# Attention outputs stored with channels as rows: transposes moved from TensorE to VectorE in a parallel attention and MLP block

## The chip, the cores and the metric

The kernel runs on one core of one Trainium2 chip. The metric is device time in microseconds (us), the median of several executions. Trace rows name the engines PE (TensorE, matmuls), PEld (its weight loads), DVE (VectorE), ACT (ScalarE), POOL (GpSimd) and SP (SyncE, which here only issues DMAs). A "q" behind an engine means its instruction queue: SPq rows are DMA issues.

## The reference

The input x is 2048 tokens of 576 channels in float32. It is layer-normed once, and two branches are added to it: a sliding, dilated attention (32 heads of 18 channels; each token sees 8 keys at distances 0, 2, ..., 14) with an output projection, and a dense layer with Mish between 576 and 4608 channels.

```python
xn = layernorm(x)
q, k, v = split_heads(xn @ wqkv)                  # 32 heads of 18
logits = einsum("bhsd,bhswd->bhsw", q, kg) * 18 ** -0.5   # kg: keys at pos - 2*w, w < 8
o = einsum("bhsw,bhswd->bhsd", softmax(logits), vg)
attn = o.reshape(1, 2048, 576) @ wo
h = xn @ w1 + b1
mlp = (h * tanh(softplus(h))) @ w2
out = x + attn + mlp
```

## The kernel before

Tokens are handled in two halves `hf` of 1024 (`SH`). Token `p * 8 + j` of a half lies on partition p (128) in row group j (`TJ` = 8). Every float32 matrix product is made from a high part in fp32r and a low part (the remainder), three products for one; most of the large products also go by a seven-product scheme over 2x2 blocks, which is why the code forms sums and differences of operands (S1 to S4, T1 to T4).

The order of the work is written out by hand. `add` appends items to `plan`, each a stretch of TensorE work (a QKV item, a part of the first dense product, a pair of the second, a part of the output projection); `before` hangs other work in front of an item (loads, casts, steps of attention). At the end every engine's instructions are chained in that order, so each engine and SP's one DMA queue run strictly in program order: an instruction that waits holds all behind it on its queue.

Attention is a generator (`attention`, line 511) advanced at chosen items. It handles the 16 head-pair units of a half two at a time, eight pairs in each half, 16 in all. For each pair POOL multiplies queries and keys, VectorE reduces them to logits, softmax follows, POOL multiplies by the values (`pv`), and VectorE reduces these into `og`, a tile of 128 partitions by 8 row groups by 72 channels (line 582). After the last of the four reductions of a pair, SP stores `og` in the DRAM buffer `o_d` (line 584), with tokens as rows: 1024 pieces of 72 floats. The first half's pairs end between 142 and 636 us, the second half's between 706 and 1058.

The output projection runs last: eight blocks p of 256 tokens (row groups j and j + 1 of a half; blocks 0 to 3 are the first half). `o_load` (line 880) brings row group j as a tile `o` of 128 tokens by 576 channels, with the last 64 channels doubled behind, in two DMAs. `o_split` (line 888) turns it and prepares the operands for TensorE in steps: step 0 takes row group j + 1 into `t1`, step 1 takes row group j into `t0` and the last channels of both into `tr_`, each by TensorE transposes of 128x128 into PSUM; ScalarE casts the high parts (A, B, S), VectorE and POOL form the sums and the low parts. The steps of block p + 1 are placed inside the three parts of block p (`wo_part`, line 1042); block 0's stand ahead, among the last items of the dense layer. Each part multiplies into one of three PSUM banks h1, h3, h2 and VectorE adds the result to the output tile (`acc`, line 1064); h1 is multiplied into again after it has been read, so a product there waits for the addition before it. SP loads block p + 2's tiles while block p runs, and sends the finished rows out. `A` and `B` of successive blocks share a ring of three buffers ("wb").

Of the kernel before, what the change touches and what calls it, by code (L numbers as in the profile page):

```python
# [8 lines left out]
F32 = mybir.dt.float32  # L9
# [30 lines left out]
def block_kernel(ctx: ExitStack, tc: tile.TileContext, x, wq, wo, w1, b1, w2, mask, out):  # L40
# [470 lines left out]
    def attention(hf):  # L511
# [9 lines left out]
        for pair in range(NQ * UQ // PU):  # L521
            n = f"{hf}_{pair}"
            vs, nxt = [], []
            L = sb.tile([P, PU, TJ, W, 2], F32, tag="L", bufs=2, name=f"L_{n}")
            hj = TJ // 2
            for k, (kt, q) in enumerate(kqs):
                for c in range(2):
                    flush()
                    pr = sb.tile([P, hj, W, CU], F32, tag="pr", bufs=2, name=f"pr_{n}_{k}_{c}")
                    j0 = c * hj  # L530
                    hh = hj // 2
                    on = hf and pair == 0
                    if on:
                        nc.vector.tensor_tensor(
                            out=pr, in0=q[:, j0:j0 + hj, None, :].to_broadcast([P, hj, W, CU]),
                            in1=win(kt, 0, CU, j0, hj), op=ALU.mult)
                    for x in () if on else range(0, hj, hh):
                        nc.gpsimd.tensor_tensor(  # L538
                            out=pr[:, x:x + hh], in0=q[:, j0 + x:j0 + x + hh, None, :].to_broadcast([P, hh, W, CU]),
                            in1=win(kt, 0, CU, j0 + x, hh), op=ALU.mult)  # L540

                    def red(pr=pr, k=k, j0=j0, L=L):
                        nc.vector.tensor_reduce(  # L543
                            L[:, k, j0:j0 + hj].rearrange("p j w h -> p (j w h)"),
                            pr.rearrange("p j w (h d) -> p (j w h) d", h=2), axis=AX, op=ALU.add)
                    behind[0] = red
                    if k == 0:
                        vs.append(load_kv(hf, pair * PU + c, 1))
                    yield
            flush()  # L550
            if hf == 0:
                lm = L[0:2].rearrange("p k j w h -> p k (j w h)")
                nc.vector.tensor_add(lm, lm, mk[:, None, :].to_broadcast([2, PU, TJ * W * 2]))
            m = sb.tile([P, PU * TJ, 2], F32, tag="m", bufs=2, name=f"m_{n}")
            Lf = L.rearrange("p k j w h -> p (k j) w h")
            Lt = Lf.rearrange("p j w h -> p j h w")
            nc.vector.tensor_reduce(m, Lt, axis=AX, op=ALU.max)
            mb = m[:, :, None, :].to_broadcast([P, PU * TJ, W, 2])
            nc.vector.tensor_sub(Lf, Lf, mb)
            Ls = L.rearrange("p k j w h -> p (k j w h)")  # L560
            if (hf, pair) == (0, 4):
                soon.append(lambda: nc.scalar.preload_act_table_set("natural_log_exp_and_others"))
            soon.append(lambda Ls=Ls: nc.scalar.activation(Ls, Ls, AF.Exp, scale=SCALE))
            if (hf, pair) == (0, 4):
                soon.append(root1)
            yield
            nc.vector.tensor_reduce(m, Lt, axis=AX, op=ALU.add)
            nc.vector.reciprocal(m, m)
            nc.vector.tensor_mul(Lf, Lf, mb)  # L569
            og = sb.tile([P, TJ, PU * CU], F32, tag="og", bufs=1, name=f"og_{n}")  # L570
            for k, vt in enumerate(vs):
                for h in range(2):
                    flush()
                    pr = sb.tile([P, TJ, DH, W], F32, tag="pr", bufs=2, name=f"pv_{n}_{k}_{h}")
                    for x in range(0, TJ, hj):
                        nc.gpsimd.tensor_tensor(  # L576
                            out=pr[:, x:x + hj].rearrange("p j d w -> p j w d"),
                            in0=L[:, k, x:x + hj, :, h:h + 1].to_broadcast([P, hj, W, DH]),
                            in1=win(vt, h * DH, DH, x, hj), op=ALU.mult)

                    def red(pr=pr, og=og, c0=k * CU + h * DH, last=(k, h) == (PU - 1, 1), pair=pair):
                        nc.vector.tensor_reduce(og[:, :, c0:c0 + DH], pr, axis=AX, op=ALU.add)  # L582
                        if last:
                            nc.sync.dma_start(
                                o_d[hf][:, pair * PU * CU:(pair + 1) * PU * CU]
                                .rearrange("(p j) c -> p j c", j=TJ), og)
                    behind[0] = red
                    if (hf, pair, k, h) == (0, *(4, 0, 1)):
                        newton1()
                    if k == 0 and (pair + 1) * PU + h < NQ * UQ:  # L590
                        nxt.append(load_kq(hf, (pair + 1) * PU + h))
                    yield
            kqs = nxt
        flush()
        yield

    ASTEPS = NQ * UQ // PU * 9

# [281 lines left out]
    def o_load(hf, j):  # L880
        if j >= TJ or (hf, j) in os_:
            return
        o = os_[hf, j] = sb.tile([P, 5 * P], F32, tag="xn", bufs=XNB, name=f"o_{hf}_{j}")
        ov = o_d[hf].rearrange("(p j) d -> p j d", j=TJ)[:, j, :]
        nc.sync.dma_start(o[:, 0:D], ov)
        nc.sync.dma_start(o[:, D:D + 64], ov[:, KT * P:D])

    def o_split(p, step, early=False):
        hf, j = divmod(2 * p, TJ)
# [12 lines left out]
        H = 2 * P  # L902
        if step == 0:
            src = os_[hf, j + 1]
            for k in range(KT):
                nc.tensor.transpose(t1[:, k * P:(k + 1) * P], src[:, k * P:(k + 1) * P], ident)
            a21 = od["a21"] = sb.tile([P, H], F32, tag="mn", bufs=5, name=f"a21_{p}")
            nc.scalar.copy(a21, t1[:, 0:H])
            s1 = od["s1"] = sb.tile([P, 2, H], F32, tag="mn", bufs=5, name=f"s14_{p}")
            nc.vector.tensor_tensor(out=s1[:, 0], in0=t1[:, H:2 * H], in1=a21, op=ALU.add)  # L910
            a22 = t1[:, H:2 * H].rearrange("p (k t) -> p k t", k=2)
            nc.scalar.copy(B[:, 0], a22)
            nc.vector.tensor_sub(B[:, 1], a22, B[:, 0].bitcast(F32))
            return
        a1, s1 = od["a21"], od["s1"]
# [2 lines left out]
        rr = tr_[:, 0:H].rearrange("p (k t) -> p k t", k=2)  # L918
        if step == 1:
            src = os_[hf, j]  # L920
            for k in range(KT):
                nc.tensor.transpose(t0[:, k * P:(k + 1) * P], src[:, k * P:(k + 1) * P], ident)
            for k in range(2):
                nc.tensor.transpose(tr_[:, k * P:(k + 1) * P], os_[hf, j + k][:, KT * P:], ident)
            s2 = od["s2"] = sb.tile([P, 2, H], F32, tag="mn", bufs=5, name=f"s23_{p}")
            nc.vector.tensor_tensor(out=s2[:, 0], in0=s1[:, 0], in1=t0[:, 0:H], op=ALU.subtract)
            nc.vector.tensor_tensor(out=s2[:, 1], in0=t0[:, 0:H], in1=a1, op=ALU.subtract)
# [199 lines left out]

    kv_d = [dram.tile([2 * UQ, HALO + S, CU], F32, name=f"kv_d{g}") for g in range(NQ)]
    q_d = [dram.tile([UQ, S, CU], F32, name=f"q_d{g}") for g in range(NQ)]
    o_d = [dram.tile([SH, D], F32, name=f"o_d{h}") for h in range(NH)]  # L1130
    y_d = dram.tile([SH, D], F32, name="y_d")

    def rest_loads():
# [455 lines left out]
```

## Time and profile before

| | |
|---|---|
| time, three runs | 1119.57 us median (1119.29 to 1120.29) |
| profiled execution | span 1118.2 us from the first to the last instruction, 18402 instructions; the profile has no other time of it |
| SP's stores of `og` | 16, 0.51 to 0.76 us each to issue |
| SP's loads of `o` | 32 (two for each of 16 tiles), 0.32 to 0.78 us each to issue |
| TensorE transposes of `o` | 80, in lines 906, 922 and 924 |
| DMA | 271.08 MB, 147487 packets, of which 30114 under 512 B |

In a profile's group rows ("line engine op out<-in ... xcount | busy, mean ns | idle before"), the middle is the total busy time in us and the mean of one in ns; the end is the time for which the engine stood idle just before these instructions and what ended most of it. Waiting lists read "who line <- what it waited for: us in total, times, longest". The chain in order of time and the timeline start each row with the start in us and the length in us; equal neighbours are merged, with their count behind an x. A row by source has min/median/max in ns.

### The profile page before, as it was taken

To read this page: it belongs to the slowest core of one execution; us is meant where nothing else is said; L and a number is where in the kernel's file an instruction comes from. 1 tells how busy PE (TensorE), PEld (TensorE's weight loads), DVE (VectorE), ACT (ScalarE), POOL (GpSimd) and SP (SyncE) were. 2 spreads that over 40 slices of the span, in tenths; PEclk is the share of its full clock that TensorE was granted. 3 is DMA by queue.
4 is the path that set the end of the run, shared out by engine and by line. 5 is a ranking of instruction groups with operands and counts; after the bars stand their busy time and mean duration, and the time that the engine had idled before them with its cause. 6 is when DMAs were issued, how large, how long until landed. Compare 5 with 4: busy or idle time off the path is not lost.

```text
span 1118.2 us, 18402 instructions
## 1 busy us (share of the span) xinstructions
PE 1109.2 (99%) x6630; PEld 1023.9 (92%) x6630; DVE 835.2 (75%) x1355; ACT 491.7 (44%) x892; POOL 777.4 (70%) x631
## 2 busy tenths in 40 slices
PE   8999999999999999999999999999999999999998
PEld 8999899999999999999999888989999999999998
DVE  6369788888888888887656566687866677776876
ACT  5544645544554545555233354343433343443332
POOL 2479777767689687685787346666789878668632
PEclk9999999999999999999999999999999999999999
DMA  6899695868767849666696797665655477576463
GB/s 200 284 311 313 227 357 205 294 227 282 260 241 265 273 169 342 226 240 215 208 332 234 240 378 254 225 200 188 220 192 190 173 266 270 207 258 243 160 217 108
DMA packets 147487, 271.08 MB, mean 242 GB/s; under 512 B 30114, under 2 KB 86724, under 8 KB 147396
## 3 DMA queue, kind: packets, MB, share of 16 engines
q1 hardware_dynamic: 147396, 269.91, 69.8%
q8 instruction: 52, 0.85, 0.3%
q14 instruction: 39, 0.32, 0.1%
HBM read 160.39 MB, written 109.48 MB: 241 GB/s over the span
## 4 chain that ended last, share of the span: by engine, by line
PE 94%; DVE 3%; POOL 1%; ACT 1%; issue 1%; DMA 0%; SPq 0%; DVEq 0%; POOLq 0%; ACTq 0%
PE h L661 30%; PE po L759 20%; PE pq L348 11%; PE po L872 10%; PE po L851 7%; PE h L667 6%; PE o L1060 4%; PE z L446 4%; POOL accP L860 1%; DVE accP L875 0%; POOL act L713 0%; DMA acc<-in_x 0%; PE ta L75 0%; DVE og L582 0%; POOL act L814 0%
## 5 line engine op out<-in xcount | busy, mean ns | idle before, releaser
L759 PEld LDWEIGHTS po<-w,act 128*128 128x128 f32 x1728 | 236.4, 188 | 6.0 <-POOL act L713 0.4
L759 PE MATMUL po<-w,act 128*128 128x288 f32 x1728 | 240.7, 295 | 0.1
L576 POOL TENSOR_TENSOR pv<-L,kv 128x576 f32<-128x576 f32 x128 | 176.3, 1477 | 38.5 <-DVE L L569 28.9
L713 POOL TENSOR_TENSOR act<-c,act 128x512 fp32r<-128x512 f32 x81 | 107.6, 1329 | 126.1 <-ACT act L712 124.4
L538 POOL TENSOR_TENSOR pr<-q,kv 128x576 f32<-128x576 f32 x120 | 184.2, 1564 | 7.7 <-DMA q<-q_d 6.0
L763 DVE TENSOR_TENSOR acc<-po,acc 128x288 f32<-128x288 f32 x288 | 120.0, 449 | 31.8 <-PE po L759 30.5
L348 PE MATMUL pq<-wq,xt 128*128 128x432 f32 x672 | 136.4, 361 | 1.2 <-ACT xt L81 1.2
L872 PEld LDWEIGHTS po<-w,act 128*128 128x128 f32 x960 | 131.1, 188 | 3.7 <-DVE accP L875 0.4
L872 PE MATMUL po<-w,act 128*128 128x288 f32 x960 | 133.8, 295 | 0.2
L348 PEld LDWEIGHTS pq<-wq,xt 128*128 128x128 f32 x672 | 125.0, 188 | 8.2 <-ACT xt L81 2.1
L707 ACT ACTIVATE c<-c,b1c 128x512 f32<-128x512 f32 x81 | 58.7, 725 | 130.6 <-DVE c L706 130.2
L661 PE MATMUL h<-S,t 128*128 128x512 f32 x432 | 110.4, 391 | 0.0
L661 PE MATMUL h<-xt,t 128*128 128x512 f32 x432 | 110.4, 391 | 0.0
L695 ACT COPY c<-h 128x512 f32<-128x512 f32 x81 | 47.5, 586 | 133.2 <-PE h L667 75.2
L582 DVE TENSOR_REDUCE og<-pv 128x144 f32<-128x1152 f32 x64 | 85.9, 1343 | 26.8 <-POOL pv L576 26.7
L661 PE MATMUL h<-xt,wa 128*128 128x512 f32 x432 | 104.1, 390 | 0.0
L543 DVE TENSOR_REDUCE L<-pr 128x64 f32<-128x1152 f32 x64 | 85.8, 1342 | 17.6 <-POOL pr L538 17.4
L875 DVE TENSOR_TENSOR accP<-po,accP 128x288 f32<-128x288 f32 x160 | 69.7, 454 | 38.9 <-PE po L872 37.4
L661 PEld LDWEIGHTS h<-xt,wa 128*128 128x128 f32 x432 | 80.9, 188 | 17.0
L851 PEld LDWEIGHTS po<-pw,u 128*128 128x128 f32 x672 | 92.2, 188 | 2.9 <-DVE u L805 0.7
L851 PE MATMUL po<-pw,u 128*128 128x288 f32 x672 | 93.7, 295 | 0.4 <-DVE u L805 0.4
L661 PEld LDWEIGHTS h<-xt,t 128*128 128x128 f32 x432 | 79.1, 188 | 14.7 <-DVE rt L706 0.2
(232 smaller groups left out, 1848.7 us busy)
## 6 DMA issues: line engine op xcount, KB each, us to landing
kv<-kv_d SPq DMA_DIRECT2D x64, 396.0 KB, 5.6
kept_t<-t SPq DMA_DIRECT2D x36, 512.0 KB, 5.2
t<-kept_t SPq DMA_DIRECT2D x36, 512.0 KB, 5.0
rw<-in_w SPq DMA_DIRECT2D x36, 320.0 KB, 4.5
kept_wa<-wa SPq DMA_DIRECT2D x18, 640.0 KB, 4.7
kept_w<-w SPq DMA_DIRECT2D x20, 576.0 KB, 4.1
wa<-kept_wa SPq DMA_DIRECT2D x18, 640.0 KB, 6.3
w<-kept_w SPq DMA_DIRECT2D x20, 576.0 KB, 4.7
```

What stands on the lines that cost most here:

```text
L348: nc.tensor.matmul(pq[:, 0:432], XT[:, xi, tok], wt[wi][:, hl, 0:432], start=i == 0, stop=i == len(seq) - 1)
L538: nc.gpsimd.tensor_tensor(out=pr[:, x:x + hh], in0=q[:, j0 + x:j0 + x + hh, None, :].to_broadcast([P, hh, W, CU]), in1=win(kt, 0, CU, j0 + ...
L543: nc.vector.tensor_reduce(L[:, k, j0:j0 + hj].rearrange("p j w h -> p (j w h)"), pr.rearrange("p j w (h d) -> p (j w h) d", h=2), axis=AX, ...
L576: nc.gpsimd.tensor_tensor(out=pr[:, x:x + hj].rearrange("p j d w -> p j w d"), in0=L[:, k, x:x + hj, :, h:h + 1].to_broadcast([P, hj, W, DH]),
L582: nc.vector.tensor_reduce(og[:, :, c0:c0 + DH], pr, axis=AX, op=ALU.add)
L661: nc.tensor.matmul(ph, wt[:, wl, wk * P:(wk + 1) * P], X[:, xs, :], start=first and i == 0, stop=last and i == len(seq) - 1, skip_group_ch ...
L713: nc.gpsimd.tensor_tensor(out=a[:, 1, :], in0=t, in1=a[:, 0, :].bitcast(F32), op=ALU.subtract)
L759: nc.tensor.matmul(po, acts[hf, q, b, j][:, al, tok], done["w2", hf, 2 * q + j][:, wl, c * HC:(c + 1) * HC], start=i == 0, stop=i == 5)
L763: nc.vector.tensor_tensor(out=t, in0=po, in1=t, op=ALU.add)
L851: nc.tensor.matmul(po, units[e, k, qq][:, al, tok], w[:, qq, wl, :], start=i == 0, stop=i == 5)
L872: nc.tensor.matmul(po, acts[hf, q, b, j][:, al, tok], done["w2", hf, 2 * q + j][:, wl, c * HC:(c + 1) * HC], start=i == 0, stop=i == 5)
L875: nc.vector.tensor_tensor(out=t, in0=po, in1=t, op=ALU.add)
```

## The change

`og` is no longer stored as it is. A new function `o_send` turns it on VectorE in 32x32 blocks into a tile `oT`: read in the order channel, then row group, 32 columns (4 channels by 8 row groups) of 32 partitions become 32 partitions by 32 tokens. Four DMAs, one for each 32 partitions of `og`, store it in `o_d`, whose layout is now channel, row group, token. `o_load` therefore brings channels on partitions: 512 channels by one DMA and the last 64 twice by two. In `o_split` TensorE's transposes are gone. ScalarE copies the loaded tile into the same PSUM tiles `t1` (the upper half only), `t0` and `tr_`; `a21`, which was copied out of PSUM, is now a view of the loaded tile, and B's high part is cast from the loaded tile too. All later steps are the same.

```diff
-                            nc.sync.dma_start(
-                                o_d[hf][:, pair * PU * CU:(pair + 1) * PU * CU]
-                                .rearrange("(p j) c -> p j c", j=TJ), og)
+                            o_send(hf, pair, og)
...
+    def o_send(hf, pair, og):
+        oT = sb.tile([P, PU * CU * TJ], F32, tag="oT", bufs=1, name=f"oT_{hf}_{pair}")
+        nc.vector.transpose(oT.rearrange("p (c j) -> p c j", j=TJ), og.rearrange("p j c -> p c j"))
+        rows = o_d[hf][pair * PU * CU:(pair + 1) * PU * CU].rearrange("(n c) j p -> (c j) n p", c=4)
+        for g in range(4):
+            part = slice(g * 32, (g + 1) * 32)
+            nc.sync.dma_start(rows[:, :, part], oT[part].rearrange("i (n k) -> i n k", k=32))
...
-        ov = o_d[hf].rearrange("(p j) d -> p j d", j=TJ)[:, j, :]
-        nc.sync.dma_start(o[:, 0:D], ov)
-        nc.sync.dma_start(o[:, D:D + 64], ov[:, KT * P:D])
+        nc.sync.dma_start(o[:, 0:KT * P].rearrange("p (k t) -> p k t", k=KT),
+                          o_d[hf][0:KT * P, j, :].rearrange("(k p) t -> p k t", p=P))
+        for r_ in range(2):
+            nc.sync.dma_start(o[r_ * 64:(r_ + 1) * 64, KT * P:], o_d[hf][KT * P:D, j, :])
...
             src = os_[hf, j + 1]
-            for k in range(KT):
-                nc.tensor.transpose(t1[:, k * P:(k + 1) * P], src[:, k * P:(k + 1) * P], ident)
-            a21 = od["a21"] = sb.tile([P, H], F32, tag="mn", bufs=5, name=f"a21_{p}")
-            nc.scalar.copy(a21, t1[:, 0:H])
+            nc.scalar.copy(t1[:, H:2 * H], src[:, H:2 * H])
+            a21 = od["a21"] = src[:, 0:H]
...
-            nc.scalar.copy(B[:, 0], a22)
+            nc.scalar.copy(B[:, 0], src[:, H:2 * H].rearrange("p (k t) -> p k t", k=2))
...
             src = os_[hf, j]
-            for k in range(KT):
-                nc.tensor.transpose(t0[:, k * P:(k + 1) * P], src[:, k * P:(k + 1) * P], ident)
+            nc.scalar.copy(t0, src[:, 0:KT * P])
             for k in range(2):
-                nc.tensor.transpose(tr_[:, k * P:(k + 1) * P], os_[hf, j + k][:, KT * P:], ident)
+                nc.scalar.copy(tr_[:, k * P:(k + 1) * P], os_[hf, j + k][:, KT * P:])
...
-    o_d = [dram.tile([SH, D], F32, name=f"o_d{h}") for h in range(NH)]
+    o_d = [dram.tile([D, TJ, P], F32, name=f"o_d{h}") for h in range(NH)]
```

## The prediction

> **What bounds the kernel now.** I read the page's busy shares first, then the chain of work that ended last, then TensorE's waits, and then the engines by stretch: the change touches the end of the run most, and shares over the whole span would hide that.
>
> ```profile
> span 1118.2 us, 18402 instructions
> PE 1109.2 (99%) x6630; PEld 1023.9 (92%) x6630; DVE 835.2 (75%) x1355; ACT 491.7 (44%) x892; POOL 777.4 (70%) x631
> ...
> PE 94%; DVE 3%; POOL 1%; ACT 1%; issue 1%; DMA 0%; SPq 0%; DVEq 0%; POOLq 0%; ACTq 0%
> ...
> 400.00:500.00 100.00, 100.00 (x611) 91.73 (x610) 84.56 (x129) 49.74 (x83) 82.47 (x71) 1.00 0.68 248
> ...
> 1040.50:1058.30 17.80, 16.40 (x123) 15.60 (x122) 16.69 (x36) 3.71 (x9) 12.24 (x10) 1.00 0.35 128
> 1066.10:1105.20 39.10, 39.10 (x303) 38.76 (x301) 29.43 (x71) 13.72 (x30) 12.94 (x10) 1.00 0.56 180
> ...
> PE o L1060 <- DVE y L1064: 1.3, 2, 0.7
> ```
>
> The numbers behind each stretch are its length and then the busy times of PE, PEld, DVE, ACT and POOL, the granted clock, the DMA share and GB/s. TensorE is the bound: 99% busy, 94% of the chain, at full clock. One stretch is different. From 1040.5 to 1058.3 TensorE is busy 16.40 of 17.80 us and VectorE 16.69: the last attention pair, the last additions of the dense layer and the start of the output projection all meet on VectorE there, and TensorE's two waits for the projection's additions fall at its end. From 1066.1 to 1105.2 TensorE never rests.
>
> **What goes: 80 transposes on TensorE.** Each of the eight projection blocks p has 4 + 4 + 2 of them (lines 906, 922, 924).
>
> ```profile
> L906 PE MATMUL ot<-ident,o x32: 270/273/273, 1040.6 to 1102.5; 128*128 128x128 f32 x32
> ...
> 1034.42 3.19 PE po L872 x24
> ...
> 1066.28 4.79 PE o L1060 x36
> ...
> 1105.29 9.66 PE o L1060 x72
> ...
> 1070.64 0.43 PE L1060 MATMUL o<-wo_r,ob 128*128 128x288 f32 x2
> 1070.91 0.60 PE L906 MATMUL ot<-ident,o 128*128 128x128 f32 x4
> 1071.26 1.83 PE L1060 MATMUL o<-wo,oS 128*128 128x288 f32 x12
> ```
>
> The 273 ns is a latency, not a price, because they are pipelined. The price comes from the period. From the chain, 1066.28 to 1105.29 are five blocks: 39.01 / 5 = 7.80 us each. A block has 50 matmuls of 288 columns (6+8+6+8+6+8+8 in wo_part), and 24 such take 3.19 us, 0.133 each: 6.64 us. So ten transposes cost 7.80 - 6.64 = 1.16 us, with what they delay behind them (the last three rows: four hold TensorE from 1070.91 to 1071.26). All eight sets together are 8 x 1.16 = 9.3 us, the most that can be won. Six sets (those of blocks 2 to 7, placed inside blocks 1 to 6) lie where TensorE never waits: 6 x 1.16 = 7.0 us. The sets of blocks 0 and 1 lie in the stretch held by VectorE.
>
> **Whether VectorE can follow a shorter block.** Once the transposes are gone, TensorE's third product in h1 waits only for the addition that reads h1 (acc(1, 0)), and ahead of that on VectorE stand s1 and B's low part.
>
> ```profile
> L1064 DVE TENSOR_TENSOR y<-o,y 128x288 f32<-128x288 f32 x18 | 8.0, 453 | 2.0 <-PE o L1060 1.8
> L1064 DVE TENSOR_TENSOR accP<-o,accP 128x288 f32<-128x288 f32 x18 | 7.9, 453 | 2.4 <-PE o L1060 2.2
> L932 DVE TENSOR_TENSOR oa<-ot,oa 128x512 fp32r<-128x512 f32 x5 | 3.5, 691 | 0.4
> L936 DVE TENSOR_TENSOR ob<-ot,ob 64x256 fp32r<-64x256 f32 x5 | 2.1, 427 | 0.2
> L910 DVE TENSOR_TENSOR s<-ot,a 128x256 f32<-128x256 f32 x5 | 2.1, 425 | 2.5 <-ACT a L908 2.5
> L913 DVE TENSOR_TENSOR ob<-ot,ob 128x256 fp32r<-128x256 f32 x5 | 2.1, 424 | 2.2 <-ACT ob L912 2.2
> L927 DVE TENSOR_TENSOR s<-ot,a 128x256 f32<-128x256 f32 x5 | 2.1, 416 | 0.0
> L935 DVE TENSOR_TENSOR s<-ot,s 128x256 f32<-128x256 f32 x5 | 2.1, 415 | 0.0
> L926 DVE TENSOR_TENSOR s<-s,ot 128x256 f32<-128x256 f32 x5 | 2.0, 410 | 0.0
> ```
>
> VectorE has 29.43 / 5 = 5.89 us of work in a block, under TensorE's 6.64. Its idle time in five blocks is 2.0 + 2.4 us on TensorE and 2.5 + 2.2 us on ScalarE's copies of the transposed PSUM. The latter should go: s1 takes a21 from the loaded tile, and B's high part is cast from it too. B's cast may still not start before the second product has read A of the block before (ring "wb" of 3), so in order: second product done about 2.1 us into the block (14 x 0.133 and the latency), its addition, s1, B's low part and acc(1, 0) follow, 0.45 + 3 x 0.43 us, to 3.8 to 3.9, where TensorE wants to go on at 28 x 0.133 = 3.7 us. I put 0.1 us of wait into each block, from 0 to 0.2: 6 x (1.16 - 0.1) = 6.4 us won.
>
> **What ScalarE gets.** It copies t1's upper half (256 columns), t0 (512) and tr_ (2 x 128) into PSUM, and loses the copy a21.
>
> ```profile
> L928 ACT CAST oa<-ot 128x512 fp32r<-128x512 f32 x5 | 2.9, 586 | 9.8 <-DVE s L927 9.8
> ...
> L908 ACT COPY a<-ot 128x256 f32<-128x256 f32 x5 | 1.9, 372 | 9.5 <-PE ot L906 9.5
> ...
> L86 ACT CAST xt<-tb 128x128 fp32r<-128x128 f32 x5 | 1.4, 271 | 0.0
> ```
>
> No row copies out of SBUF into PSUM; by size, from rows that read PSUM, 372 + 586 + 2 x 271 - 372 = 1.1 us per block more, on 13.72 / 5 = 2.7: 3.9 of 6.7 us. Twice the price would make it 5.4, still under TensorE. I cost it at nothing; the cover is ScalarE's idle 9.8 and 9.5 us in five blocks.
>
> **The transposes on VectorE, 16 of 128x576.** They stand behind the last reduction of each pair, so VectorE is held for both in one go.
>
> ```profile
> L312 DVE TENSOR_TENSOR twT<-twT,twhT x16: 740/752/1841, 130.5 to 298.2; 128x576 fp32r<-128x576 f32 x16
> ...
> L582 DVE TENSOR_REDUCE og<-pv x64: 1298/1344/1355, 101.7 to 1056.5; 128x144 f32<-128x1152 f32 x64
> ```
>
> The profile has no such transpose. The same number of elements takes 0.74 us in an addition; twice as many take 1.34 in a reduction, the upper end. I take 0.75, since one operand of 576 is nearest to the first, in all 12 us; the reductions, which read one operand, keep their time (1298 to 1355), while that addition is stretched to 1841 at worst. [...]
>
> In the first 1040 us a late VectorE is covered by four banks of PSUM: at 400 to 500 us it is busy 84.56 of 100 us and TensorE still all of it. One wait of 0.75 can use that cover up where a round is tight; I put 0.05 us on each of 15 places, 0.8 us in all, between 0 and 15 x 0.75 = 11.
>
> In the stretch held by VectorE the last transpose is on the path:
>
> ```profile
> DVE ob L913 <- ACT ob L912: 0.9, 2, 0.4
> ...
> 1056.46 1.34 DVE L582 TENSOR_REDUCE og<-pv 128x144 f32<-128x1152 f32 x1
> 1057.72 0.81 DVE L1064 TENSOR_TENSOR y<-o,y 128x288 f32<-128x288 f32 x2
> ...
> 1058.32 0.90 PE L1060 MATMUL o<-wo,oS 128*128 128x288 f32 x5 [0.69 <-DVE y L1064]
> ```
>
> TensorE goes on at 1058.32 because the addition at 1057.72 came late. The new instruction stands between the reduction and that addition: +0.75. The first row is VectorE's waiting list from 1040 to 1058.5: two waits of 0.44 for B's cast, blocks 0 and 1, which go: -0.88. Net 0.1 us won, and the 2 x 1.16 us of TensorE's time in this stretch bring nothing. Bounds: -0.7 (waits stay) to +2.2 (TensorE's earlier start draws VectorE along).
>
> **Stores and loads on SP's queue.** A pair's store becomes four, of 576 rows of 128 B each instead of 1024 rows of 288 B; a load becomes three, 640 rows of 512 B instead of 256.
>
> ```profile
> L584 SPq DMA_DIRECT2D o_d<-og x16: 513/519/755, 142.4 to 1057.8; - x16
> DMA to landing us min/median/max: 3.1/3.4/7.8
> ...
> SPq L584 <- DVE og L582: 72.8, 13, 10.5
> ...
> q1 hardware_dynamic: 147396, 269.91, 69.8%
> ...
> 849.84 0.43 SPq L282 DMA_DIRECT2D t<-kept_t  x1
> ...
> 871.76 1.52 PE L661 MATMUL h<-xt,t 128*128 128x512 f32 x6
> ...
> 1071.44 0.38 SPq L885 DMA_DIRECT2D o<-o_d  x1
> ...
> 1078.73 0.60 PE L906 MATMUL ot<-ident,o 128*128 128x128 f32 x4
> ```
>
> SP already stands at these stores waiting for VectorE (72.8 us); whatever is queued behind comes 0.75 + 3 x 0.52 = 2.3 us later, sixteen times: kv loads and weight fetches. These are issued a round ahead: the fetch at 849.84 lands about 5 us later and its tile is read from 871.76 on. I cost it at nothing. Packets rise by 16 x (2304 - 1024) + 16 x (640 - 256) = 26,600; at the mean packet's share, 0.698 x 16 x 1118.2 us / 147,396 = 85 ns, that is 141 us on each engine's account, an upper bound since the mean packet is 1.8 KB and the bytes stay equal. In the projection a block's tile is issued at 1071.44 and first needed at 1078.73. It will go out some 0.7 us later (its main load is the fourth of six instead of the third of four) and be needed 1.1 us sooner: 5.5 us for a landing of 3.4. Covered, with 2 us to spare; the output stores queued behind gain two issues a block ahead of them, and no one waits for those. The last pair's four stores are issued to about 1061 and land near 1064; block 4, the first to read them, loads at about 1070.
>
> **Sum.** 6.4 + 0.1 - 0.8 = 5.7 us off the profiled execution: 1118.2 to 1112.5 us of span. The median of the runs shown is 1.4 us over that span; kept, it gives 1119.6 - 5.7 = 1113.9 us.
>
> **Rivals.** *Both ends gain:* VectorE's wait in the stretch at 1040 us was itself due to TensorE's late start, so two more sets count, 2.2 in place of 0.1: 7.8, and without the loop's cost 8.6: 1111. Against it: VectorE is busy 16.69 of 17.80 there. *VectorE takes over as the bound:* 14 instructions of a block at their single times (7 x 0.453 and the seven others, 3.2: 6.4 us) and waits on TensorE of 4.4 / 5 = 0.9, so 7.3 to 7.5 us for a block: 6 x 0.4 = 2.4 won, less 0.7 at 1058 and 0.8 in the loop: 1118.7, no change. For it: 5.89 of 6.64 is close; against: back to back they overlap. [...] *Slower, by SP's queue:* if the four issues hold it longer (0.755 each, 3 us with the transpose), or rows of 128 B land late beside engines that are already 69.8% taken, fetches behind them miss their round. It decides where a fetch has under 3 us of slack. Were half the 16 places to cost TensorE 1.5 us: +12 - 6.4 = +5.6, 1125. Against it: no wait of TensorE on a DMA now. *The transpose is not the short instruction assumed,* 2.7 us or several: 43 us more on VectorE, 2 lost at 1058, 15 x 0.4 in the loop: 1121.
>
> **From these to the numbers.** A measurement of this kernel tells about 0.2%, 2.2 us, from no change. Forecast 0.63, with its own range 1111.5 to 1117; both ends gain 0.07; VectorE the bound 0.13; SP's queue 0.11; a long transpose 0.06, half of it within 2.2 us of before. Faster 0.70, same 0.16, slower 0.14. The range for eight in ten reaches into the cases at both sides: 1110.5 to 1121.
>
> **What will show it.** Blocks of 6.6 to 6.9 us in the chain, instead of 7.80; 16 DVE transposes near 0.75 us; no wait of VectorE on ScalarE at lines 910 and 913; block 0's third product still starting at about 1058; no TensorE wait released by DMA. It is wrong if the block's period stays above 7.3, if TensorE's busy share before 1040 us falls, or if ScalarE waits for the loads.

## The result, and the profile after

The kernel after takes 1118.18 us (median of 20 executions, 1116.62 to 1118.93), the kernel before 1119.64 us (20 executions beside it, 1119.27 to 1120.29). The ratio is 0.9984, with a 95% interval of 0.9978 to 0.9991. The change won 1.5 us; 5.7 us were forecast. The profiled execution took 1116.71 us, with a span of 1114.9 us.

The page of the kernel after, its busy times, DMA queue and chain:

```profile
span 1114.9 us, 18235 instructions
PE 1100.3 (99%) x6550; PEld 1013.6 (91%) x6550; DVE 852.4 (76%) x1371; ACT 497.9 (45%) x916; POOL 776.8 (70%) x631
...
q1 hardware_dynamic: 175044, 269.91, 70.9%
...
PE 87%; DVE 4%; POOL 3%; DMA 2%; ACT 1%; issue 1%; SPq 1%; DVEq 0%; ACTq 0%; POOLq 0%
```

TensorE lost its 80 transposes and is still 99% busy, but its part of the chain fell from 94% to 87%: VectorE, GpSimd and DMAs now stand in between. The packets rose by 27,600 and the queue's share by 1.1 points only, so the narrow rows are cheap in transfer time.

TensorE's waits after (who, for what, us in total, times, longest):

```profile
PE o L1064 <- DVE y L1068: 2.1, 2, 1.0
PE o L1064 <- issue: 2.0, 1, 2.0
...
PE h L667 <- DVE rt L712: 0.7, 1, 0.7
PE z L446 <- DVE zqs L459: 0.7, 1, 0.7
```

The list of before had 1.3 us for the first of these and none of the other three. (One more is new: 0.5 us for an addition at 1046.10. It stands in the run without the transposes too, and not in the run with the transposes alone.) Where they stand is seen in the timeline of after, VectorE's and TensorE's rows (start, length, in brackets the idle time before and its releaser):

```profile
591.67 1.35 DVE L582 TENSOR_REDUCE og<-pv 128x144 f32<-128x1152 f32 x1 [1.50 <-POOL pv L576]
593.06 1.33 DVE L597 STREAM_TRANSPOSE oT<-og 128x576 f32<-128x576 f32 x1
...
595.60 1.44 PE L446 MATMUL z<-z_B,S 128*128 128x432 f32 x6 [0.68 <-DVE zqs L459]
...
1055.87 1.86 PE L1064 MATMUL o<-wo,oS 128*128 128x288 f32 x12 [1.02 <-DVE y L1068]
...
1059.98 1.03 PE L1064 MATMUL o<-wo,oS 128*128 128x288 f32 x6 [1.99 <-issue]
...
1079.64 1.86 PE L1064 MATMUL o<-wo,oS 128*128 128x288 f32 x12 [1.03 <-DVE y L1068]
```

There are three kinds of loss. In the loop (595.60; a second one ends at 780.73) a reduction of 1.35 us and a transpose of 1.33 stand back to back on VectorE, as behind every pair, and here TensorE waits for an addition behind them. In block 0 the third product starts at 1059.98 instead of 1058.32, after a rest of 1.99 us. In block 3 a new wait of 1.03 us ends at 1079.64.

The transposes' own row, by source (min/median/max in ns):

```profile
L597 DVE STREAM_TRANSPOSE oT<-og x16: 1208/1328/1371, 139.4 to 1058.3; 128x576 f32<-128x576 f32 x16
```

The engines by stretch after, the five block periods from 1066.68 to 1101.83 and the stretch held by VectorE (columns as in the prediction):

```profile
1066.68:1101.83 35.15, 34.08 (x253) 33.43 (x251) 28.25 (x70) 17.84 (x45) 12.94 (x10) 1.00 0.67 209
1040.50:1059.98 19.48, 15.96 (x114) 14.91 (x113) 19.12 (x40) 5.82 (x16) 12.34 (x11) 1.00 0.48 147
```

Taking a block from the third product of one to the third product of the next, the six periods are 6.70, 6.98, 7.94, 6.73, 6.75 and 6.75 us, 41.85 together. Before they were 46.83. VectorE, with 19.12 of 19.48 us, holds the end of the loop harder than before (16.69 of 17.80).

Comparing the starts of the same products in the two profiled executions gives the ledger (minus is won):

| part | forecast | measured |
|---|---|---|
| start-up | 0 | -0.4 |
| loop: two new waits of TensorE | +0.8 | +1.7 (0.77 and 0.94) |
| 1040 us to block 0's third product | -0.1 | +0.3 |
| the six block periods | -6.4 | -5.0 |
| span | -5.7 | -3.3 |

The start-up's 0.4 us is not the change's: the profile of a kernel that differs only in later loads has a start-up 0.4 us longer than the one of after. The ledger holds 2.4 us of the shortfall of 4.3. Another 0.4 lies in the way from span to time. The forecast added 1.4 us, a median of three runs less the span of another execution; the 88 executions of the kernel before beside the experiments stand 1.7 to 1.9 us over their own spans, as the changed kernel's do. The last 1.5 us are not in this execution: 13 of the 20 show a mean granted clock of 0.998 instead of 1.0 and are 1.5 us longer (median 1118.44 against 1116.93 for the other seven).

### The profile page after: what moved, and what is told of

It reads as the page before. It is cut to its first block, busy times and chain, and to the rows that moved or that the text cites. A ratio compares the mean times of both kernels' runs of the same rounds, so it can differ in the third digit from the quotient of the medians.

```text
span 1114.9 us, 18235 instructions
## 1 busy us (share of the span) xinstructions
PE 1100.3 (99%) x6550; PEld 1013.6 (91%) x6550; DVE 852.4 (76%) x1371; ACT 497.9 (45%) x916; POOL 776.8 (70%) x631
## 4 chain that ended last, share of the span: by engine, by line
PE 87%; DVE 4%; POOL 3%; DMA 2%; ACT 1%; issue 1%; SPq 1%; DVEq 0%; ACTq 0%; POOLq 0%
PE h L667 29%; PE po L765 21%; PE pq L348 9%; PE po L878 9%; PE po L857 7%; PE h L673 6%; PE o L1064 4%; PE z L446 3%; DMA o<-o_d 1%; POOL pv L576 1%; POOL s L618 1%; DVE og L582 1%; POOL accP L866 1%; DMA wo<-wkept_B 1%; POOL act L719 0%
```

## The experiments

Theory A: the transposes cost through VectorE, which comes late with what TensorE waits for. Theory C: the rests so made bring TensorE's clock down. Theory D: the narrow stores on SP's queue make the loss. Theory Y: block 3's wait comes from the place of the y loads in SP's queue (they bring back from DRAM the sums of the first half's tokens, onto which VectorE adds the projection in blocks 0 to 3). Line numbers in the rows are those of each kernel's own listing and differ by a few.

**The changed kernel, profiled again.** No edit.

> The changed kernel once more, as the yardstick of this chip. Its runs so far fall into two groups: 1116.6 to 1117.8 us where the mean granted clock of TensorE is 1.0, and 1118.0 to 1118.9 where it is 0.998. Theory C (TensorE's two long rests in block 0, 3 us together, now and then let the granted clock fall): both groups again, and in a profile with 0.998 the clock falls between 1056 and 1070 us. Rival (the clock falls anywhere, by chance): the fall lies elsewhere, or the kernel before shows it as often.

It took 1118.14 us (ratio 0.9986, 0.9977 to 0.9995), and its profile caught the clock. The engines by stretch around it:

```profile
1058.20:1061.61 3.41, 1.47 (x11) 1.50 (x12) 3.23 (x7) 0.45 (x1) 0.00 (x0) 1.00 0.25 39
1061.61:1065.02 3.41, 3.41 (x16) 3.41 (x15) 2.39 (x6) 2.24 (x7) 2.11 (x2) 0.50 0.54 136
```

From 1061.61 to 1065.02 TensorE runs at half the clock and issues 16 matmuls; at the full clock a stretch of that length without a rest has 28 (the last row of the fence on the grid, below). The products behind come 1.5 us late. The stretch just ahead holds block 0's rest: TensorE is busy for 1.47 of 3.41 us. The kernel before shows a clock of 0.998 in 2 of its 88 executions beside these runs.

**The transposes alone**, in the kernel before, their result unused:

```diff
+                            oT = sb.tile([P, PU * CU * TJ], F32, tag="oT", bufs=1, name=f"oT_{hf}_{pair}")
+                            nc.vector.transpose(oT.rearrange("p (c j) -> p c j", j=TJ), og.rearrange("p j c -> p c j"))
```

> The kernel before with the 16 VectorE transposes added and their results unused; stores, loads and TensorE's transposes as before. Theory A (the changed kernel's losses come from VectorE being held 1.33 us instead of 0.75 behind each pair): 1.3 to 2 us more than before, about 1121.3, with the new waits of TensorE near 595 us (for z's sums) and 779 us (for line 706's sum) as in the changed kernel, and block 0's third product about 1.3 us later. Rival D (the losses before 1040 us come from four narrow stores on SP's queue): no new wait at 595 and 779, within 0.5 us of before but for block 0.

1122.86 us, ratio 1.0032 (1.0019 to 1.0045). TensorE's waits:

```profile
PE o L1062 <- DVE y L1066: 2.5, 2, 1.9
...
PE h L663 <- DVE rt L708: 0.7, 1, 0.7
PE z L446 <- DVE zqs L459: 0.7, 1, 0.7
```

The stores, the loads and the projection are those of before, and yet the two waits of the loop are there (the products behind them start 0.85 and 1.01 us later), block 0's third product starts 1.36 us later, and a clock fall follows in this profile. So the losses in the loop and in block 0 are VectorE's.

**Everything but the transposes**, the changed kernel storing `og` as it lies (its channels come out in a wrong order):

```diff
-        oT = sb.tile([P, PU * CU * TJ], F32, tag="oT", bufs=1, name=f"oT_{hf}_{pair}")
-        nc.vector.transpose(oT.rearrange("p (c j) -> p c j", j=TJ), og.rearrange("p j c -> p c j"))
+        oT = og.rearrange("p j c -> p (j c)")
```

> The changed kernel with the VectorE transposes left out: the four stores send og's bytes as they lie, so the attention outputs are in the wrong places. Theory A: the waits near 595 and 779 us go (1.65 us), block 0's third product starts 1.3 to 2 us sooner: about 3 us under the full-clock runs of the changed kernel, 1114. Theory C: no run with clock 0.998, so all runs near 1114. Rival D: the waits at 595 and 779 stay, gain of 1.3 us in block 0 alone.

1113.97 us, ratio 0.9948 (0.9932 to 0.9965). TensorE's waits:

```profile
PE o L1063 <- DVE y L1067: 1.7, 2, 1.0
...
PE o L1063 <- issue: 0.8, 1, 0.8
```

The loop's two waits are gone, with the same 64 narrow stores on SP's queue: theory D falls. Block 0's rest is 0.8 us instead of 2.0, and none of the four executions has a low clock. The 16 transposes cost 1118.14 - 1113.97 = 4.2 us in all, or 2.9 against the three executions above that had the full clock (median 1116.85); 0.75 + 0.8 us were priced.

**The last pair's transpose and stores moved to the start of block 1.**

```diff
-                        if last:
+                        if last and (hf, pair) == (1, NQ * UQ // PU - 1):
+                            last_send.append(lambda: o_send(hf, pair, og))
+                        elif last:
                             o_send(hf, pair, og)
...
+    before(at["o", 1, 0], lambda: last_send.pop()())
```

> The changed kernel, but the last pair's transpose and its four stores stand at the start of projection block 1 instead of behind the last reduction; nothing is left out. Theory A: block 0's third product no longer waits for it, 1.3 us less, of which up to 0.6 comes back in block 1 where VectorE has little to spare: 0.7 to 1.3 us under the changed kernel. Theory C: TensorE's long rest of 2 us goes with it, so the group with clock 0.998 vanishes: median 1116 or less. Without C both groups stay, each about 1 us lower.

1119.47 us, ratio 0.9996 (0.9987 to 1.0005): nothing won. TensorE's timeline:

```profile
1059.16 1.03 PE L1068 MATMUL o<-wo,oS 128*128 128x288 f32 x6 [0.77 <-issue]
...
1074.51 3.15 PE L1068 MATMUL o<-wo,oS 128*128 128x288 f32 x12 [2.84 <-DVE y L1072]
```

Block 0's rest shrinks to 0.77 us, as it should. But a rest of 2.84 us appears in block 2, and the clock falls behind it. The four stores, 2.0 us on SP's queue, now stand ahead of block 1's loads; the y loads for block 2 go out at 1070.02 instead of 1067.94. That they are what VectorE waited for is argued from these starts; the profile names no releaser.

**Matmuls in place of the rest.** Twelve plain matmuls, whose output is not used, behind block 0's second part:

```diff
             mul(h3, S3, "T3", True, more=((1, r1),))
+            if p == 0:
+                for n in range(12):
+                    nc.tensor.matmul(h2, S3[:, 0, n % 2], wo_t["T3"][:, 0, n % 2], start=True, stop=True,
+                                     skip_group_check=True)
             acc(1, 1, h3)
```

> The changed kernel with 12 more plain matmuls behind block 0's second part (into the accumulator of A12 B21, which has been read by then; its output is not used again), so that TensorE works through 1.6 us of the 1.99 us rest that ends at 1059.98, and nothing else moves: the third product still waits for VectorE and starts at 1060.0. Theory C (the rests of 1.0 and 2.0 us bring the clock down to one half for 3.4 us in some executions): no execution shows the low clock after block 0, all of them lie near the 1116.6 to 1117.8 us that those without it had, median 1116.9. Rival (the clock falls by itself, at a place that only happens to lie there): the runs still fall into two groups, median 1118.1. Rival (added matmuls hold up the third product): it starts later than 1060.2 and the time is above 1118.5.

1117.34 us, ratio 0.998 (0.9971 to 0.999). TensorE works more and the median is 0.8 us lower, though the ratios to the kernel before, 0.998 and 0.9984, cannot be told apart. What the run shows clearly is the clock: the only low one in ten executions is at start-up (9.90 to 13.32 us), where the changed kernel had 20 in 30. Theory C holds, and the traces give its size. The changes of the clock, those at the start and the end of a run too, lie whole multiples of 3.41 us apart (in the second profile of the changed kernel 1054.72, 3.41 and 51.20 us, which are 309, 1 and 15 times 3.4133; in the profiles of before and after 1112.75 us, 326 times), on a grid that is placed differently in each execution; so each full stretch of that grid can be looked at. Two examples, the engines by stretch of one kernel (half-length transposes and single remainder load, below), whose grid had a rest of 1.82 us in one stretch and of 1.69 us in another:

```profile
1053.26:1056.67 3.41, 1.59 (x13) 1.36 (x12) 3.31 (x7) 1.67 (x5) 3.41 (x3) 1.00 0.10 26
1056.67:1060.08 3.41, 3.01 (x14) 2.69 (x13) 3.38 (x7) 0.00 (x0) 0.06 (x1) 0.50 0.00 0
...
1070.32:1073.73 3.41, 1.72 (x14) 1.48 (x13) 1.47 (x5) 1.86 (x6) 1.40 (x2) 1.00 0.98 331
1073.73:1077.14 3.41, 3.41 (x28) 3.41 (x27) 2.53 (x7) 0.55 (x2) 0.00 (x0) 1.00 0.53 129
```

Behind 1.82 us of rest the next stretch has half the clock, behind 1.69 us it has the full one. In all profiles here the seven stretches inside the run with 1.82 to 3.16 us of rest were followed by a fall. Of those with less only the start-up's was, with 1.71 us. Three at the very end, with 1.75, 1.76 (after, 1110.00 to 1113.41) and 1.90 us by modelled ends, were not. By these profiles the limit is put near half of the stretch, an estimate; 1.71 with a fall and 1.90 without leave it no sharper than that. Block 0's rest of 1.99 us exceeds it only when nearly all of it lies in one stretch. Counting the starts of the grid for which at least 1.8 us do gives an estimate of about 1.8 of 3.41 us, 53%. The four kernels with this rest (the changed one, and those with the y loads or the remainder's load edited alone) show a clock of 0.998 or less in 32 of 60 executions, though from 2 to 7 of ten in the single runs, so the agreement is one of the sum only. The four runs whose profile has no rest over 1.1 us in the projection (the one without transposes, the two with matmuls and y loads together, and the last, below) show it in none of 21.

**Transposes in two halves**, the first behind the second reduction of a pair, the other where the whole one stood; the stores as they were:

```diff
-                        if last:
-                            o_send(hf, pair, og)
+                        if h:
+                            o_turn(hf, pair, og, k)
+                        if (k, h) == (PU - 1, 1):
+                            o_send(hf, pair)
...
+        c = slice(k * CU, (k + 1) * CU)
+        nc.vector.transpose(oT_[hf, pair].rearrange("p (c j) -> p c j", j=TJ)[:, c],
+                            og.rearrange("p j c -> p c j")[:, c])
```

> The changed kernel with each transpose cut into two of 288 columns, the first right behind the second reduction, the other where the whole one stood; the same four stores. Theory A (what the transposes cost is VectorE's lateness at the three places where a whole one of 1.33 us stands ahead of an operation that TensorE waits for): a half takes 0.67 us, the waits at 595 and 779 fall from 0.7 and 0.9 to between 0 and 0.3, the third product of block 0 starts 0.3 to 0.7 us earlier against the work before it, and the time is 1.5 to 2.5 us below the changed kernel's: 1116.1. Rival (a transpose has a fixed part, so that two cost more than one): halves of 0.9 us or more, time 1118 or above. Rival (the wait is for the stores, or for the buffer): no change of the waits, 1118.1.

1117.83 us, ratio 0.9986 (0.9977 to 0.9996). The halves by source, and below TensorE's waits:

```profile
L604 DVE STREAM_TRANSPOSE oT<-og x32: 694/748/778, 112.1 to 1059.6; 128x288 f32<-128x288 f32 x32
```

```profile
PE o L1075 <- DVE y L1079: 3.5, 2, 1.8
...
PE o L1075 <- issue: 1.5, 1, 1.5
```

The two waits of the loop are out of the list (the products there start 0.59 and 0.55 us earlier against the work before them), so they were VectorE's lateness by one long instruction. But it is no gain: the earlier halves add new delays of 0.4 us at 113, 0.6 at 833 and 0.8 ahead of 1057.12, block 3's wait is 0.6 us longer (1.66), and two halves take 1.50 us where one whole takes 1.33. The expected 1116.1 was missed. A low clock does not always cost time here: seven of the ten executions have it, and three of these are the fastest of all (1116.74 to 1117.18). Where their falls lie is not shown, since the profile is of an execution at full clock.

**One DMA for the remainder's rows** (a token tile's last 64 channels, wanted twice) instead of two, alone and with the halves:

```diff
-        for r_ in range(2):
-            nc.sync.dma_start(o[r_ * 64:(r_ + 1) * 64, KT * P:], o_d[hf][KT * P:D, j, :])
+        rem = o_d[hf][KT * P:D, j, :]
+        nc.sync.dma_start(o[:, KT * P:], bass.AP(tensor=rem.tensor, offset=rem.offset,
+                                                 ap=[[0, 2]] + [list(a) for a in rem.ap]))
```

> The changed kernel with the remainder's rows loaded by one DMA into both halves of the partitions, instead of by two: SP issues 2 loads for a token tile instead of 3, 1.2 us less for a block. Theory Y (block 3's 1.03 us wait at 1079.64 comes from y loads that stand behind six o loads on SP's queue): the y loads issue at 1074.7, the wait falls to 0.1 or less, that block takes 6.8 us instead of 7.94, and the time is 1.0 us below the changed kernel's: 1117.1. Rival (the y loads are slow because of the transfer itself, which shares the DMA engines with the o loads): they land at 1079.0 all the same and the time stays at 1118.1.

> Both edits, the halved transposes and the single load of the remainder. If the two waits are independent the gains add: 1.0 + 2.0 us below the changed kernel's, 1115.1. If block 0's rest falls below what brings the clock down, the 0.9 us that it costs on the average goes as well: 1114.3. If the y loads' wait only hides VectorE's lateness, the gain is that of one of the two: 1116 to 1117.

1118.58 us (ratio 0.9993, 0.9984 to 1.0003) and 1118.47 us (0.9992, 0.9982 to 1.0001): not faster than the changed kernel, against the expectation. Eight of the ten executions with the single load alone are without the low clock, and these take 1118.50 us (median), 1.6 more than the changed kernel's of that kind. The timeline with the single load, SP and TensorE:

```profile
1066.62 2.19 SPq L1040 DMA_DIRECT2D y<-y_d  x2
...
1073.32 1.87 PE L1065 MATMUL o<-wo,oS 128*128 128x288 f32 x12 [1.60 <-DVE y L1069]
```

The y loads go out at 1066.62, 1.3 us earlier than after, but take 2.19 us to issue, and VectorE adds onto the rows they bring only from 1072.81. The profile names no releaser there, so that it waited for these loads is argued. Fewer loads ahead on SP's queue are thus not enough. Why the single load makes its followers slow stays open.

**The y loads between the o loads**, first on SP's queue, then on GpSimd's at their old place:

```diff
-        if k < TJ:
-            before(at["o", k // 2 - 1, 1], lambda k=k: y_load(k))
+        if k in (6, 8):
+            before(at["o", k // 2 - 2, 0], lambda k=k: (y_load(k - 2), y_load(k - 1)))
```

```diff
-        nc.sync.dma_start(ys[j][:, 0:D], y_d.rearrange("(p j) d -> p j d", j=TJ)[:, j, :])
+        (nc.sync if j < 4 else nc.gpsimd).dma_start(ys[j][:, 0:D], y_d.rearrange("(p j) d -> p j d", j=TJ)[:, j, :])
```

> The changed kernel with the y loads of a block (the query half's sums that VectorE adds onto) issued between the two token tiles' o loads, not behind both. Theory Y1 (the 1.03 us wait at 1079.64 goes by the place of the y loads in SP's queue): they issue at 1073.3 instead of 1075.9 and land at 1076.8, the wait goes, the sum of the four blocks from block 1's start falls by 1.0 us, and the time with it: 1117.1. Rival Y2 (what stands in SP's queue is carried out at a pace that the transfers set, as with the single load of the remainder, whose y loads issued 1.3 us earlier and landed 1.5 us later): the wait moves to another block, of 0.6 us or more, and the time stays at 1118.1. Rival Y3 (the second o tile, now 1.0 us later, is wanted as early): a wait of about 1 us for an o load in its place.

> The changed kernel with the last four y loads on GpSimd's queue, so that they stand behind no o load. Theory Y1: they issue as soon as their buffers are free (about 1066 and 1073), land within 4 us, the wait at 1079.64 goes, 1117.1. Rival Y2 (the transfers set the pace): the y loads share the engines with the o loads, a wait of 0.6 us or more is left in block 2 or 3, 1118.1. Rival Y4 (GpSimd's issue waits for the buffer, and the additions behind it on GpSimd come late): a new wait of TensorE for GpSimd.

On SP's queue 1116.21 us, ratio 0.9972 (0.9963 to 0.9981); on GpSimd's 1117.82 us, 0.998 (0.997 to 0.9989), of whose ten executions seven had the low clock and the other three took 1115.43 to 1116.22. The chain after and one row of VectorE's waiting list show what the wait was, and TensorE's timeline with the first edit what is left of it:

```profile
1071.36 0.49 ACT ot L926
...
1074.43 1.43 SPq L893
1075.86 0.04 issue
1075.90 3.13 DMA y<-y_d
...
DVE y L1068 <- DMA y<-y_d: 1.1, 1, 1.1
```

```profile
1060.77 1.03 PE L1064 MATMUL o<-wo,oS 128*128 128x288 f32 x6 [1.99 <-issue]
1083.01 1.04 PE L1064 MATMUL o<-wo,oS 128*128 128x288 f32 x6 [0.36 <-ACT ot L928]
```

After, ScalarE's copy frees the o tile, six o loads follow one another on SP's queue, the last of them takes 1.43 us, and the y loads go out last, at 1075.90. With the y loads between the o loads the 1.03 us wait is gone and 0.36 us for an o tile takes its place; the periods of 6.98 and 7.94 us become 6.74 and 7.27. Theory Y holds, for 0.8 us among the executions without the low clock (medians 1116.93 and 1116.16). The rest of the lower median is luck as far as is known: three of the ten executions have the low clock, against 13 of 20.

**The last pair's stores on GpSimd's queue**, with its transpose at the start of block 1, as in the run that moved both:

```diff
+                            last_send.append(lambda: o_send(hf, pair, og, nc.gpsimd))
...
-    def o_send(hf, pair, og):
+    def o_send(hf, pair, og, queue=nc.sync):
...
-            nc.sync.dma_start(rows[:, :, part], oT[part].rearrange("i (n k) -> i n k", k=32))
+            queue.dma_start(rows[:, :, part], oT[part].rearrange("i (n k) -> i n k", k=32))
```

> The changed kernel with the last pair's transpose at the start of block 1, as in the run before that had it so, and its four stores on GpSimd's queue, so that SP's loads do not stand behind them. If the 2.84 us rest that the earlier run had before 1074.51 came from its loads behind those stores, it goes: the rest of block 0 falls to 0.8 us (no clock fall follows), block 3 keeps the changed kernel's 1.0 us wait, and the time is 1116.0. If it came from VectorE's transpose in block 1 itself, a rest of over 2 us stays in block 1 or 2 and the time is 1118 or more.

1121.78 us, ratio 1.0018 (1.0008 to 1.0027), far from the expected 1116.0. GpSimd's timeline:

```profile
1064.19 0.88 POOL L605 DMA_DIRECT2D o_d<-oT  x1 [0.47 <-DVE oT L601]
1067.52 0.68 POOL L605 DMA_DIRECT2D o_d<-oT  x1 [2.45 <-issue]
1071.32 0.67 POOL L605 DMA_DIRECT2D o_d<-oT  x1 [3.12 <-issue]
1073.88 0.67 POOL L605 DMA_DIRECT2D o_d<-oT  x1 [1.89 <-issue]
1074.56 1.27 POOL L945 TENSOR_TENSOR oS<-s,oS 128x512 fp32r<-128x512 f32 x1
```

Four issues take from 1064.19 to 1074.55. The low part of S, which GpSimd computes behind them, comes late, and TensorE waits 4.4 us for it; block 0's rest is 0.77 us, as expected. What the 2.84 us of the run before came from, this run does not tell. What held each issue for 2 to 3 us the profile does not name. The end of VectorE's work did not release the last one: VectorE's last instruction ahead of it ends at 1072.35, 1.5 us before the issue at 1073.88.

**The added matmuls and the y loads between the o loads together** (both diffs above), and once more beside further executions of the kernel before:

> The 12 added matmuls and the y loads between the o loads together. With theory C (no clock fall in block 0) and theory Y1 the gains add: 1117.3 - 1.0 = 1116.3. With rival Y2 the time stays at 1117.3.

> The 12 added matmuls with the y loads between the o loads once more, beside the kernel before on the same chip, for a narrower interval: 1116.3, and no execution with the clock fall after block 0.

1116.34 us (0.9968, 0.9956 to 0.9981) and 1116.32 us (0.9967, 0.9955 to 0.998). None of the eleven executions has the low clock, and the time is the expected one. The y loads between the o loads alone had 1116.21 us, with three low clocks in ten; so what the matmuls add to them is seen in the clock and not in the median.

**The last pair's transpose at the start of block 1, its stores behind block 1's loads, with the y loads between the o loads:**

```diff
+    lp = 1, NQ * UQ // PU - 1
+    before(at["o", 1, 0], lambda: last_send.append(o_turn(*lp, last_send.pop())))
     for k in range(4, 2 * TJ):
...
+        if k == 7:
+            before(at["o", 1, 0], lambda: o_send(*lp, last_send.pop()))
```

> The changed kernel with the y loads between the o loads (as before) and the last pair's transpose at the start of block 1, its four stores on SP's queue behind block 1's loads. Theory A+Y1 (block 0's rest of 2.0 us is the transpose that stands ahead of its second part's additions; the two earlier tries lost only by what their stores held up): the rest falls to 0.8 us, no execution shows the clock fall there, and the time is 0.5 to 1.0 us below the 1116.1 us that the y loads' edit alone had in its executions without the fall: 1115.4. Rival Q (the four stores, 2.0 us of issue wherever they stand on SP's queue, hold up what comes behind: now block 1's stores of the output, whose buffers block 3's y loads take): a rest of 1 us or more in block 3, 1116.4 or more. Rival V (the transpose in block 1 is as much in VectorE's way as in block 0): a rest of 0.6 us or more in block 1, and the time stays at 1116.2 to 1116.7.

1116.29 us, ratio 0.9969 (0.9957 to 0.9981), no low clock in six executions. TensorE's timeline, and then SP's:

```profile
1058.71 1.03 PE L1071 MATMUL o<-wo,oS 128*128 128x288 f32 x6 [0.77 <-issue]
...
1064.31 1.86 PE L1071 MATMUL o<-wo,oS 128*128 128x288 f32 x12 [0.60 <-DVE y L1075]
...
1080.82 1.03 PE L1071 MATMUL o<-wo,oS 128*128 128x288 f32 x6 [0.89 <-ACT ot L935]
```

```profile
1073.29 2.04 SPq L1046 DMA_DIRECT2D y<-y_d  x2
1075.38 0.43 SPq L897 DMA_DIRECT2D o<-o_d  x1
1075.85 1.16 SPq L900 DMA_DIRECT2D o<-o_d  x2
```

The rest of block 0 falls to 0.77 us, so it was the transpose's place. A wait of 0.60 us appears in block 1, where VectorE now does that work (rival V). And one of 0.89 us appears in block 3, where rival Q put it. There ScalarE's first copy for block 4, at 1079.09, stood 1.99 us waiting for an o load, and the second o tile is issued behind the y loads, at 1075.38. With the y loads' edit alone the same copy waited 1.46 us. Whether the four stores made it longer is not shown. The 2.84 us rest in block 2 does not come back, though VectorE's transpose stands where it stood with that rest: so it came from the order on SP's queue.

These three versions, at 1116.2 to 1116.3 us, beat the kernel before by 0.3% and, by their ratios to it, the changed kernel by 0.12 to 0.17%. They differ from one another by less than can be told. The one with the y loads alone is the simplest; its executions still fall into two groups.

## Why the prediction was wrong

The time came out 4.3 us above the forecast. By the ledger, rounded, 1.4 of it lie in the blocks, 0.9 in the loop and 0.4 at 1040 us; 1.5 are the clock's and 0.4 the step from span to time, less the 0.4 of a shorter start-up. Two steps failed: the y loads were left out of "Covered", and the transpose was priced at 0.75 us and takes 1.33. The clock was no step at all.

**The blocks: right in mechanism, short by a missing load.** "I put 0.1 us of wait into each block" gave 6.74 us; the four undisturbed periods are 6.70, 6.73, 6.75 and 6.75. ScalarE's copies took 0.37, 0.58 and 2 x 0.27 us, as priced, and ScalarE is busy for 17.84 / 5 = 3.57 us of a block, hiding them. VectorE's waits for ScalarE at the old lines 910 and 913 went (3.0 and 2.6 us from 1062 to 1105 us before), and ScalarE waits for no load. But 6.4 us became 5.0, because two periods are 6.98 and 7.94. The failed step is "Covered, with 2 us to spare". It counted the o loads, for which it held (TensorE waits for none of them after), and not the y loads, which stand behind all six of them. Before, they left 3.3 us after the start of blocks 1 and 2, the second pair at 1072.39; after, 5.0 and 6.3 us, the second pair at 1075.90. The expectation "no TensorE wait released by DMA" held by the letter only: the wait is shown as one for VectorE, which waited for the load.

**The transpose's price: the failed step that cost most,** since the loop's waits and block 0's long rest hang on it. "I take 0.75, since one operand of 576 is nearest to the first" chose the addition's row; the instruction takes 1.33 us, the reduction's row at the other end of the bound. With 1.33 the stretch at 1040 us comes to 1.33 - 0.88 = 0.45 lost, and 0.3 was measured. The waits for B's cast there did go, and without the transposes the third product starts 1.23 us sooner against the work before it, which would leave 0.9 won, as the rest of that sum had it.

**The loop: mis-sized.** "0.05 us on each of 15 places" should have been nothing at thirteen and 0.8 to 0.9 us at two. At all of them a reduction and a transpose together hold VectorE for 2.7 us; at the two, an addition that TensorE needs soon stands behind them. At the others TensorE shows no new wait; that the banks of PSUM cover them is argued. With half-length transposes these two waits go, and with no transposes too.

**The clock: absent from the prediction.** "At full clock" was read from a kernel whose longest rest in the stretch was 0.69 us. The forecast asked what a later third product costs, 0.75 us, and not whether the longer rest would slow what follows. It costs 1.5 us in 13 of 20 executions, enough to move the median.

**SP's queue: right for the stores.** Its 64 narrow stores are issued in 0.5 us each, land in 2.0, and cost nothing before the projection. The rival by which they would cost 12 us fell with the run without transposes. Its remark on the output stores, "no one waits for those", holds after.

The rival that came nearest to the time is VectorE as the bound (1118.7), and it is wrong as to the place: the blocks are not held by VectorE. Nearest in mechanism is the transpose that is "not the short instruction assumed": it was priced at 2.7 us, twice what it takes, but the loss at 1058 us and in the loop is where it put it. Without transposes the change gives 1119.57 - 1113.97 = 5.6 us. That this is near the forecast of 5.7 is luck: without the 0.75 + 0.8 us for the transposes the forecast would have been 7.25.

## What to carry to other kernels

Work that moves from the bounding engine to one with idle time is not free where that engine already holds the bound one: look for the stretches where it is busy nearly all the time (before the change 16.69 of 17.80 us), and for the places where something that the bounding engine needs soon is queued behind the moved instruction (at 595 us VectorE came late although it had just stood idle for 1.50 us). Price the instruction by the dearest plausible row, since two long instructions back to back (here 1.35 and 1.33 us) delay everything queued behind them. When loads in a queue become more, list every load behind them, not only those that the change touches. And when a rest grows, ask whether it is now long enough to bring the clock down: here that cost 1.5 us, where the rest had grown by 1.3, from 0.69 to 1.99.

## What was not expected of the hardware

TensorE's clock was 0.50 behind each of the seven stretches of a 3.41 us grid, inside a run, that held 1.82 to 3.16 us of rest, and stayed so for the next stretch (in one of the seven for two: that execution's mean clock is 0.996, where the six others have 0.998); the changed kernel therefore shows two groups of times 1.5 us apart (medians 1118.44 and 1116.93). With twelve useless matmuls that fill the rest one of ten executions has a low clock, at start-up, against 20 of 30, and the median was 0.8 us lower.

A VectorE transpose of 128x576 float32 takes 1.33 us, one of 128x288 takes 0.75: from these two sizes an estimate of 2.0 ns for each column and 0.17 us fixed. The rows of a y load issued 1.3 us earlier were used 1.5 us later when one DMA of 128 rows stood ahead of it instead of two of 64. And four DMAs issued by GpSimd took over 10 us, with 2 to 3 us between one and the next.
